# A convolution octet's inverse step joined to the next octet's forward steps, with ScalarE and VectorE each emptying one PSUM bank

## The chip, the cores and the metric

The kernel runs on one core of a Trainium2 chip. The metric is the device time of one launch in microseconds (us). Before the change it is 359.0 us, the median of three runs (358.95 to 359.44).

## The reference

Two branches share one layer norm and are added to the input. Branch A is a gated long convolution over the sequence, done in the reference by an FFT of twice the sequence length; branch B is a dense layer, Mish, and a second dense layer. There are S = 2048 rows, D = 448 channels and F = 1792 hidden columns, all in float32.

```python
def _A_ref(q, k, v, shift_k, ssm_k, ssm_D):
    k_pad = jnp.pad(k, ((0, 0), (ks - 1, 0), (0, 0)))
    k_shift = jnp.zeros_like(k)
    for t in range(ks):                                   # ks = 4
        k_shift = k_shift + k_pad[:, t:t + S, :] * shift_k[:, ks - 1 - t][None, None, :]
    kv = k_shift * v
    kv_f = rfft(pad(kv, to 2 * S), along S)
    kf_f = rfft(pad(ssm_k, to 2 * S))
    y = irfft(kv_f * kf_f)[:S]
    y = y + kv * ssm_D[None, None, :]
    return q * y

def _B_ref(x, w1, b1, w2):
    h = jnp.einsum("bsd,df->bsf", x, w1) + b1
    sp = jnp.log1p(jnp.exp(-jnp.abs(h))) + jnp.where(h > 0, h, jnp.zeros_like(h))
    act = h * jnp.tanh(sp)
    return jnp.einsum("bsf,fd->bsd", act, w2)

x = A_q
xn = _layernorm(x, axis=-1)
return x + _A_ref(xn, A_k, A_v, A_shift_k, A_ssm_k, A_ssm_D) + _B_ref(xn, B_w1, B_b1, B_w2)
```

## The kernel before

**The frame is branch B.** The sequence is cut into 8 chunks of 256 rows and the hidden columns into 7 pairs of 128, which gives 56 pairs. The program is written in slots, two to a pair. An even slot holds `g1_mm` (L494), the first dense layer of pair i: 22 matmuls of 128x256 that accumulate in one PSUM bank. An odd slot holds `mish` of that pair on ScalarE (L522), its split into a high and a low part (`ach` by a ScalarE cast, `acl` by a VectorE subtraction, L86 and L87), and `g2_mm` (L536), the second dense layer of the pair two before: 12 matmuls of 128x448. The order on every engine is the order in which the code is written. `at(slot, ...)` puts a step ahead of the slot's matmuls and `after(slot, ...)` behind them, and the loop over slots (L747) plays them in order. `dv()` lets one small waiting VectorE step through; `held` keeps a split back until `prod` calls it.

**Branch A is threaded through these slots** as a transform in steps of matmuls. Up to slot 59 the first transform step runs (L148), and its results go to DRAM (`Dh` for the filter, `Dkv` for the product of the shifted k and v). Slots 66 to 89 hold the middle step, in eight **octets** of frequencies, three slots apart (`OCT_AT`, L29), so that octets stand at even and odd slots in turn (66, 69, 72, ..., 87). Slots 100 and 108 hold the last step (L330).

An octet o consists of:

- **the forward steps**, called F(o) here: `f2_mm` (L231) four times, for the real and imaginary part of the filter (from the tile `ah`) and of the product (from `av`). One call is eight matmuls in tiles of 64x32 of the array, and each of them takes two passes, so it appears as 16 records in the trace (L237). A call fills a PSUM tile of two banks, r = 0 into the first and r = 1 into the second;
- **emptying the filter's two parts** into the SBUF tile `hs` (`h_out`), because VectorE reads only the product's parts from PSUM;
- **`prod`** (L252): four VectorE multiplications into `ya`, `yc`, `yb`, `yd` (L259), then `ya` minus `yb` (L264) and `yc` plus `yd` (L266);
- **the inverse step**, called I(o) here: `i1_mm` (L269), 16 matmuls in tiles of 32x64 with two passes each (L276), first all that read `ya`, then all that read `yc`. It fills two PSUM tiles, that is four banks;
- **`i1_out`** (L281): those four banks are emptied into `qe` and sent to the DRAM tensor `E` by a DMA of GpSimd's queue.

Three PSUM tiles of two banks serve the octets: `pp`, `pq`, `pr`, numbered 0, 1, 2. The tuples `hb`, `vb` and `ib` (L638) say which of them the filter's parts, the product's parts and the inverse step use. `GB` gives the single bank that a pair's `g1_mm` uses in these slots: bank 0 is the first of `pp`, bank 2 the first of `pq`, bank 4 the first of `pr`. `pg` is the pair of banks that `g2_mm` accumulates in. Before the change, F(o) stands at slot s of its octet and I(o-1) at slot s + 2 (at s + 1 for the last octet), and I(7) stands at slot 89.

Of the kernel before, what the change touches and what calls it, by code (L numbers as in the profile page):

```python
# [14 lines left out]
S, D, F = 2048, 448, 1792  # L15
# [5 lines left out]
NO = 8  # L21
# [23 lines left out]
def tile_kernel(ctx: ExitStack, tc, q, qT, k, v, sk, hT, sD, w10, w1, w2, c_fib, c_g, c_gi, c_i2, out):  # L45
    nc = tc.nc
    V = nc.vector
# [41 lines left out]
    def pc(n):  # L89
        return duo[n]  # L90
# [15 lines left out]
    def dv(n=1):  # L106
        for _ in range(n):
            if drip:
                drip.pop(0)()
# [4 lines left out]
    def at(slot, fn, *args):  # L114
        plan.setdefault(int(slot), []).append((fn, args))

    def after(slot, fn, *args):
        plan2.setdefault(int(slot), []).append((fn, args))
# [5 lines left out]
    HT, KR, VT, KV, PP, PS, ST, SD = {}, {}, {}, {}, {}, {}, {}, []  # L124
# [85 lines left out]
    GT, AH, AV, HS, Y = {}, {}, {}, {}, {}  # L210

    def t2(shape, name, bufs=1):
        if not sp2:
            ph1.close()
            sp2.append(ph2.enter_context(tc.tile_pool(name="ph2", bufs=1, reuse_waits="tile")))
        return sp2[0].tile(shape, F32, name=name, bufs=bufs)
# [14 lines left out]
    def f2_mm(a, o, c, n):  # L231
        p = pc(n)
        g = GT[o][0]
        for t in range(4):
            for r in range(2):
                rs = slice(64 * r, 64 * r + 64)
                nc.tensor.matmul(p[32 * t:32 * t + 32, r, :D], g[rs, t, c], a[rs, t], start=True, stop=True,  # L237
                                 tile_position=(64 * r, 32 * t))
        return p

    def hv_mm(o, hb, vb):
        PS["H", o] = [f2_mm(AH[o], o, c, hb[c]) for c in range(2)]
        h_out(o)
        PS["V", o] = [f2_mm(AV[o], o, c, vb[c]) for c in range(2)]
        AH.pop(o), AV.pop(o)

    def h_out(o):
        HS[o] = t2([128, 2, 2, D], "hs")
        for c, p in enumerate(PS.pop(("H", o))):
            nc.scalar.copy(HS[o][:, c], p[:, :, :D])  # L250

    def prod(o):  # L252
        vr, vi = (p[:, :, :D] for p in PS.pop(("V", o)))
        hs = HS.pop(o)
        hr, hi = hs[:, 0], hs[:, 1]
        a, c = Y[o] = [t2([128, 2, D], n, 2) for n in ("ya", "yc")]
        b, e = [t2([128, 2, D], n) for n in ("yb", "yd")]
        for x, *y in ((a, vr, hr), (c, vr, hi), (b, vi, hi), (e, vi, hr)):
            V.tensor_mul(x, *y)  # L259
        for fn in held:  # L260
            fn()
        held.clear()
        dv(2)
        V.tensor_sub(a, a, b)  # L264
        dv()
        V.tensor_add(c, c, e)  # L266
        dv()

    def i1_mm(o, ib):  # L269
        gi = GT[o][1]  # L270
        ps = [pc(n) for n in ib]
        for c in range(2):
            for t in range(4):
                ts = slice(32 * t, 32 * t + 32)
                for r in range(2):
                    nc.tensor.matmul(ps[t // 2][64 * r:64 * r + 64, t % 2, :D], gi[ts, r, c], Y[o][c][ts, r],  # L276
                                     start=c == 0, stop=c == 1, tile_position=(32 * t, 64 * r))
        PS["I", o] = ps
        Y.pop(o)

    def i1_out(o):  # L281
        qe = t2([128, 4, D], "qe") if o < NO - 1 else t2([128, 2, 2, D], "hs").rearrange("p a b d -> p (a b) d")
        for i, p in enumerate(PS.pop(("I", o))):
            nc.scalar.copy(qe[:, 2 * i:2 * i + 2], p[:, :, :D])  # L284
        for r in range(2):
            k = 8 * (o % 4) + 4 * r
            nc.gpsimd.dma_start(E.rearrange("p (k h) d -> p k h d", h=2)[:, k:k + 4, o // 4], qe[64 * r:64 * r + 64])  # L287
# [202 lines left out]
    AHL, P1, P2, GB = {}, {}, {}, {}  # L490
# [121 lines left out]
    for g, t in enumerate(KV_AT):  # L612
        d = t - (KV_AT[g - 1] if g else t - 6)
# [21 lines left out]
    at(OCT_AT[0], regroup)  # L635
    for o in range(NO):
        s, d = OCT_AT[0] + OCT_AT[1] * o, OCT_AT[1]
        hb, vb, ib = ((0, 1), (2, 0), (2, 1)) if s % 2 == 0 else ((2, 1), (0, 2), (0, 2))  # L638
        (at if o else after)(s - d if o else s - 7, o_load, AH, Dh, o, "ah")
        at(s - d - 1 if o else s - 3, o_load, AV, Dkv, o, "av")  # L640
        at(s, hv_mm, o, hb, vb)
        at(s, gi_load, o)
        after(s, prod, o)
        if s % 2:
            hv.add(s)
        if o == NO - 1:
            ib = 0, 1
        if o:
            at(s + (2 if o < NO - 1 else 1), i1_mm, o - 1, ib)
            after(s + (2 if o < NO - 1 else 1), i1_out, o - 1)  # L650
        if s % 2 == 0:
            GB[s // 2], GB[s // 2 + 1] = 2, 0
        else:
            GB[s // 2 + 1] = 2 if o < NO - 1 else 4
    at(s + 2, i1_mm, o, ib)
    after(s + 2, i1_out, o)
    GB[s // 2 + 2] = 5

    for t, (cs, load, folds, gates) in I2_AT.items():
        for m, (c, f) in enumerate(zip(cs, folds)):  # L660
# [56 lines left out]
    ps = [g2p.tile([128, 512], F32, name="pg2") for _ in range(2)]  # L717
# [114 lines left out]
```

## Time and profile before

| | |
|---|---|
| median of three runs | 359.0 us (358.95 to 359.44) |
| span of the profiled execution, first to last instruction | 357.0 us |
| TensorE busy | 351.0 us, 98% of the span |
| weight loads on TensorE | 289.5 us, 81% |
| VectorE busy | 270.6 us, 76% |
| ScalarE busy | 156.6 us, 44% |
| GpSimd busy | 70.3 us, 20% |
| octets (first matmul of F(0) to the first matmul behind I(7)) | 186.55 to about 284.9 us |

The page gives the span of one profiled execution. It has no separate total for that execution, so its own time is the span and what lies around it: the median of the runs is 2.0 us above the span, for start and end outside the recorded instructions. A time within the span is in microseconds from its start. In a row of the timeline the first number is the start, the second the duration, then come engine, line, operation, the tile written and the tiles read, and the number of instructions. Matmuls overlap in their pipeline, so the cost of a group of them is read from start to start, not from its duration.

### The profile page before, as it was taken

Reading aid. Unit: us, or ns where it says so; the run is one execution under the profiler, and the core shown is the slowest. Engines: PE = TensorE matmul, PEld = TensorE weight load, DVE = VectorE, ACT = ScalarE, POOL = GpSimd, SP = SyncE. Lnnn points to the kernel's source line nnn. Section 1 sums busy time; section 2 is a strip of 40 time slices with the busy share of each in tenths; the row PEclk is TensorE's granted clock in tenths of the full one; section 3 lists DMA queues with packets and bytes.
Section 4 is the critical chain, followed back from the end, with each engine's and each line's share of the span. In section 5 each row is a group of like instructions: output and inputs, shape, how many; then the busy total and the mean of one; then the engine's idle time right before and its main releaser. Section 6 shows DMA issues by size and latency. Waiting matters only on the chain.

```text
span 357.0 us, 7437 instructions
## 1 busy us (share of the span) xinstructions
PE 351.0 (98%) x3092; PEld 289.5 (81%) x3092; DVE 270.6 (76%) x375; ACT 156.6 (44%) x267; POOL 70.3 (20%) x78
## 2 busy tenths in 40 slices
PE   8999999999999999999999999999999999999995
PEld 2988888888888989888988757666775699979794
DVE  5989748999999999999437756756963933788941
ACT  4966552344243343343233454445445443354470
POOL 2037002822220240212000031011031116040030
PEclk9999999999999999999999999999999999999999
DMA  7998976949768637665869569999896387989086
GB/s 260 344 364 307 411 287 175 340 123 263 198 171 313 164 107 168 223 162 118 245 201 355 201 165 292 248 278 312 276 273 121 77 234 272 409 319 274 19 116 141
DMA packets 30691, 83.27 MB, mean 233 GB/s; under 512 B 3137, under 2 KB 15810, under 8 KB 30658
## 3 DMA queue, kind: packets, MB, share of 16 engines
q1 hardware_dynamic: 21842, 47.82, 39.4%
q0 software_dynamic: 4928, 22.95, 22.9%
q10 hardware_dynamic: 3888, 12.03, 12.8%
q8 instruction: 24, 0.39, 0.4%
q14 instruction: 9, 0.07, 0.1%
HBM read 54.34 MB, written 28.45 MB: 232 GB/s over the span
## 4 chain that ended last, share of the span: by engine, by line
PE 52%; issue 8%; DVE 6%; POOL 2%; DMA 1%
PE pq L514 7%; PE pg L546 7%; PE pg L548 7%; PE pg L547 6%; PE pp L514 5%; PE pr L514 4%; PE pp L237 3%; PE pr L237 3%; PE pp L276 2%; PE pg L514 2%; DVE x L201 2%; POOL x L184 2%; PE pq L237 2%; DMA xn<-in_qT_dram 1%; PE pr L276 1%
## 5 line engine op out<-in xcount | busy, mean ns | idle before, releaser
L546 PE MATMUL pg<-w2h,ach 128*128 128x448 f32 x224 | 82.5, 368 | 0.0
L548 PE MATMUL pg<-w2h,acl 128*128 128x448 f32 x224 | 81.4, 363 | 0.0
L547 PE MATMUL pg<-w2l,ach 128*128 128x448 f32 x224 | 81.2, 362 | 0.0
L87 DVE TENSOR_TENSOR acl<-a,ach 128x512 fp32r<-128x512 f32 x56 | 38.9, 695 | 31.7 <-ACT ach L86 31.5
L522 ACT ACTIVATE a<-pg,b1t 128x256 f32<-128x256 f32 x66 | 27.8, 472 | 65.4 <-PE pg L514 43.3
L514 PE MATMUL pg<-XH,w1h 128*128 128x256 f32 x264 | 52.6, 283 | 0.0
L546 PEld LDWEIGHTS pg<-w2h,ach 128*128 128x128 f32 x224 | 41.9, 187 | 11.5 <-issue 7.2
L514 PEld LDWEIGHTS pg<-XH,w1h 128*128 128x128 f32 x264 | 41.4, 188 | 6.9 <-issue 5.6
L547 PEld LDWEIGHTS pg<-w2l,ach 128*128 128x128 f32 x224 | 42.1, 188 | 2.4
L548 PEld LDWEIGHTS pg<-w2h,acl 128*128 128x128 f32 x224 | 42.1, 188 | 2.4
L514 PE MATMUL pg<-XL,w1h 128*128 128x256 f32 x264 | 42.9, 277 | 0.0
L158 DVE TENSOR_TENSOR st<-pq,st 128x896 f32<-128x896 f32 x32 | 34.8, 1089 | 4.8 <-ACT st L154 4.3
L514 PEld LDWEIGHTS pg<-XL,w1h 128*128 128x128 f32 x264 | 35.9, 188 | 0.0
L86 ACT CAST ach<-a 128x512 fp32r<-128x512 f32 x56 | 34.8, 622 | 1.7
L514 PE MATMUL pg<-XH,w1l 128*128 128x256 f32 x198 | 33.6, 278 | 0.0
L184 POOL TENSOR_TENSOR x<-kr,skb 128x896 f32<-128x896 f32 x8 | 17.0, 2123 | 70.9 <-PE pr L148 26.2
L514 PEld LDWEIGHTS pg<-XH,w1l 128*128 128x128 f32 x198 | 27.6, 188 | 0.2 <-DVE w1l L372 0.2
L201 DVE TENSOR_TENSOR x<-x 128x896 f32<-128x896 f32 x24 | 26.2, 1091 | 1.5 <-POOL x L184 0.8
L522 ACT ACTIVATE a<-pq,b1t 128x256 f32<-128x256 f32 x20 | 8.4, 471 | 31.8 <-PE pq L514 31.8
L287 POOL DMA_DIRECT2D E<-qe x14 | 8.7, 628 | 63.1 <-ACT qe L284 63.1
L154 ACT COPY st<-pr 128x896 f32<-128x896 f32 x16 | 14.5, 908 | 14.2 <-PE pr L148 12.3
L417 POOL TENSOR_TENSOR mv<-ve,mhalf 128x2 f32<-128x2 f32 x5 | 5.0, 1007 | 72.0 <-DVE ve L414 72.0
(138 smaller groups left out, 605.7 us busy)
## 6 DMA issues: line engine op xcount, KB each, us to landing
Dkv<-st ACTq DMA_DIRECT2D x16, 448.0 KB, 5.3
ah<-Dh SPq DMA_DIRECT2D x8, 896.0 KB, 7.5
av<-Dkv SPq DMA_DIRECT2D x8, 896.0 KB, 8.6
e<-E POOLq DMA_DIRECT2D x8, 896.0 KB, 7.2
E<-qe POOLq DMA_DIRECT2D x14, 448.0 KB, 5.9
kr<-in_k_dram SPq DMA_DIRECT2D x10, 448.0 KB, 6.8
Dh<-st ACTq DMA_DIRECT2D x10, 448.0 KB, 6.2
x<-in_hT_dram SPq DMA_DIRECT2D x8, 448.0 KB, 6.0
```

Of the source, the lines that this page charges most:

```text
L86: nc.scalar.copy(h, raw)
L87: V.tensor_sub(l, raw, h)
L154: nc.scalar.copy(st[:, 1], o)
L158: f(st[:, n], e, st[:, 1])
L184: nc.gpsimd.tensor_mul(o, KR[g - u // 2], skb[:, u:u + 1].to_broadcast([128, 2, D]))
L201: V.tensor_add(KV[g], KV[g], o)
L237: nc.tensor.matmul(p[32 * t:32 * t + 32, r, :D], g[rs, t, c], a[rs, t], start=True, stop=True, tile_position=(64 * r, 32 * t))
L514: nc.tensor.matmul(ps[n], l, r, start=all(m[0] != n for m in seq[:n_]), stop=all(m[0] != n for m in seq[n_ + 1:]))
L522: nc.scalar.activation(a[:, n], ps[n], AF.Mish, bias=b1t[:, 2 * p + n:2 * p + n + 1])
L546: nc.tensor.matmul(ps, ah[:, n, cs], w2h[:, f], start=f == 0, stop=False)
L547: nc.tensor.matmul(ps, ah[:, n, cs], w2l[:, f], start=False, stop=False)
L548: nc.tensor.matmul(ps, al[:, n, cs], w2h[:, f], start=False, stop=f == NF - 1)
```

## The change

I(o-1) is moved from slot s + 2 of octet o to the beginning of slot s, directly ahead of F(o), and the whole is one function, `octet`. The last inverse step, I(7), stays at slot 89 and is alone. Every PSUM tile of two banks that goes to SBUF (the two parts of the filter, the two results of the inverse step) is now emptied by `both`: ScalarE copies the first bank and VectorE the second, where ScalarE copied both before. `ya` and `yc` have one buffer instead of two. The bank numbers are dealt out anew: within a block the inverse step uses two of the three PSUM tiles, the filter's first part uses the third, its second part the inverse step's first tile, and so on.

```diff
-    def hv_mm(o, hb, vb):
-        PS["H", o] = [f2_mm(AH[o], o, c, hb[c]) for c in range(2)]
-        h_out(o)
+    def both(d, p):
+        nc.scalar.copy(d[:, 0], p[:, 0, :D])
+        V.tensor_copy(d[:, 1], p[:, 1, :D])
+
+    def octet(o, ib, hb, vb):
+        if o:
+            i1_mm(o - 1, ib)
+            i1_out(o - 1)
+        hs = HS[o] = t2([128, 2, 2, D], "hs")
+        ps = [f2_mm(AH[o], o, c, hb[c]) for c in range(2)]
+        for c in range(2):
+            both(hs[:, c], ps[c])
         PS["V", o] = [f2_mm(AV[o], o, c, vb[c]) for c in range(2)]
         AH.pop(o), AV.pop(o)
-
-    def h_out(o):
-        HS[o] = t2([128, 2, 2, D], "hs")
-        for c, p in enumerate(PS.pop(("H", o))):
-            nc.scalar.copy(HS[o][:, c], p[:, :, :D])
...
-        a, c = Y[o] = [t2([128, 2, D], n, 2) for n in ("ya", "yc")]
+        a, c = Y[o] = [t2([128, 2, D], n) for n in ("ya", "yc")]
...
-            nc.scalar.copy(qe[:, 2 * i:2 * i + 2], p[:, :, :D])
+            both(qe[:, 2 * i:2 * i + 2], p)
...
-        hb, vb, ib = ((0, 1), (2, 0), (2, 1)) if s % 2 == 0 else ((2, 1), (0, 2), (0, 2))
+        ib, hb, vb = ((0, 1), (2, 0), (1, 2)) if s % 2 == 0 else ((0, 2), (1, 0), (2, 1))
...
-        at(s, hv_mm, o, hb, vb)
+        at(s, octet, o, ib, hb, vb)
...
-        if o == NO - 1:
-            ib = 0, 1
-        if o:
-            at(s + (2 if o < NO - 1 else 1), i1_mm, o - 1, ib)
-            after(s + (2 if o < NO - 1 else 1), i1_out, o - 1)
-        if s % 2 == 0:
-            GB[s // 2], GB[s // 2 + 1] = 2, 0
+            GB[s // 2 + 1] = 0
         else:
-            GB[s // 2 + 1] = 2 if o < NO - 1 else 4
-    at(s + 2, i1_mm, o, ib)
+            GB[s // 2], GB[s // 2 + 1] = 0, 2
+    at(s + 2, i1_mm, o, (1, 2))
     after(s + 2, i1_out, o)
-    GB[s // 2 + 2] = 5
+    GB[s // 2 + 2] = 1
```

The line numbers of the changed kernel differ by a few: `i1_mm`'s matmuls are L280 there, `prod`'s multiplications L263, and the copies of `both` L242 (ScalarE) and L243 (VectorE).

On TensorE, before, octet 2 at slot 72 stands between the last matmul of one `g2_mm` and the first of a `g1_mm`. `ah` holds the filter, `av` the product, `g` the transform's weights.

```order
L548 MATMUL pg_2045<-w2h,acl 128x448
L237 MATMUL pp<-ah,g 32x448 x8
L237 MATMUL pq<-ah,g 32x448 x8
L237 MATMUL pr<-av,g 32x448 x8
L237 MATMUL pp<-av,g 32x448 x8
L514 MATMUL pq<-XH,w1h 128x256 x3
```

I(1) stood two slots later, at slot 74, in a place of its own.

On TensorE, in the changed kernel, the same place at slot 72:

```order
L552 MATMUL pg_2045<-w2h,acl 128x448
L280 MATMUL pp<-ya,gi 64x448 x4
L280 MATMUL pq<-ya,gi 64x448 x4
L280 MATMUL pp<-yc,gi 64x448 x4
L280 MATMUL pq<-yc,gi 64x448 x4
L237 MATMUL pr<-ah,g 32x448 x8
L237 MATMUL pp<-ah,g 32x448 x8
L237 MATMUL pq<-av,g 32x448 x8
L237 MATMUL pr<-av,g 32x448 x8
L518 MATMUL pp<-XH,w1h 128x256 x3
```

I(1) now stands directly ahead of F(2), and the second forward call writes `pp`, which I(1) filled just before.

On VectorE, before, octet 3 at slot 75: the two additions that empty `pg` into `qt`, then `prod`.

```order
L553 TENSOR_TENSOR qt<-pg_2045,qt 128x448
L259 TENSOR_TENSOR ya<-pp,hs 128x896
L259 TENSOR_TENSOR yc<-pp,hs 128x896
L259 TENSOR_TENSOR yb<-pr,hs 128x896
L259 TENSOR_TENSOR yd<-pr,hs 128x896
L87 TENSOR_TENSOR acl<-a,ach 128x512
L264 TENSOR_TENSOR ya<-ya,yb 128x896
L266 TENSOR_TENSOR yc<-yc,yd 128x896
```

On VectorE, in the changed kernel, the same place:

```order
L557 TENSOR_TENSOR qt<-pg_2045,qt 128x448
L243 COPY qe<-pp 128x448
L243 COPY qe<-pr 128x448
L243 COPY hs<-pq 128x448
L243 COPY hs<-pp 128x448
L263 TENSOR_TENSOR ya<-pr,hs 128x896
L263 TENSOR_TENSOR yc<-pr,hs 128x896
L263 TENSOR_TENSOR yb<-pq,hs 128x896
L263 TENSOR_TENSOR yd<-pq,hs 128x896
L87 TENSOR_TENSOR acl<-a,ach 128x512
L268 TENSOR_TENSOR ya<-ya,yb 128x896
L270 TENSOR_TENSOR yc<-yc,yd 128x896
```

Four copies out of PSUM stand ahead of the multiplications, two for the inverse step of the octet before and two for the filter; nothing else moved there.

## The prediction
> **What bounds the kernel now.** I read the page first, then what TensorE waited for, then the chain of work that ended last around one octet.
>
> ```profile
> span 357.0 us, 7437 instructions
> PE 351.0 (98%) x3092; PEld 289.5 (81%) x3092; DVE 270.6 (76%) x375; ACT 156.6 (44%) x267; POOL 70.3 (20%) x78
> ```
>
> A busy TensorE is not one at its peak, so the second view matters more: all that TensorE's matmuls waited for in the whole span (engine, line, the releaser, microseconds in total, times, longest).
>
> ```profile
> PE pg L696 <- DVE wz L692: 1.0, 1, 1.0
> PE pq L148 <- DVE x L204: 0.7, 1, 0.7
> PE pg L723 <- DVE ve L414: 0.2, 1, 0.2
> ```
>
> That is 1.9 us, none of it in the octets. TensorE is the bound from end to end, and a change to the octets can win only by shortening TensorE's own sequence there, and can lose by giving it a wait that it does not have. Now the chain from slot 70 to slot 72: pair 35's `g1_mm`, I(0), a `g2_mm`, F(2). A piece lasts from the end of the one before it to its own end.
>
> ```profile
> 203.16 2.51 PE pq L514 x22
> 205.67 0.54 PE pp L276 x4
> 206.20 0.03 PE pr L276 x4
> 206.23 0.35 PE pp L276 x4
> ...
> 207.33 0.03 PE pr L276 x4
> 207.36 0.40 PE pg L546
> 207.76 0.20 PE pg L547
> ...
> 209.97 0.91 PE pp L237 x16
> 210.88 0.75 PE pq L237 x16
> ```
>
> ```profile
> 213.13 2.70 PE pq L514 x22
> ```
>
> Every border between shapes costs something. I(0)'s first pass takes 0.54 where its later ones take 0.35 (entering: 0.19), and the first `g2_mm` matmul behind it takes 0.40 where the next takes 0.20 (leaving: 0.20). F(2)'s first call takes 0.91 where the second takes 0.75 (entering: 0.16), and the `g1_mm` behind it takes 2.70 where the one ahead took 2.51 (leaving: 0.19). An inverse step thus carries 0.39 us of borders and an octet's forward steps 0.35.
>
> **What the change removes.** Seven inverse steps, I(0) to I(6), lose their own place and stand directly ahead of F(1) to F(7). Each pair keeps I's entry and F's exit, and loses I's exit and F's entry: 0.20 + 0.16 = **0.36 us, seven times, 2.52 us**. What comes back is the new border inside the block and any new wait.
>
> **The new border.** No row shows a 32x64 tile followed by a 64x32 one. The bounds are nothing and the 0.20 of leaving an inverse step; I take 0.16, since the row nearest to it is the entry of these same forward matmuls. This leaves 0.20 a block. The Trainium skill, in TensorEngine Tiling, section Tiling Modes, Key Properties, says that changing the tiling mode, not just the tile, drains the array. By that rule the border between the two shapes still has its drain and the block saves 0.20; if switches between small tiles were free it would save 0.36 (rival C). The trace agrees in that all four borders above cost 0.16 to 0.20, but it has none of this kind.
>
> **The new wait.** The filter's second call now writes the tile that the inverse step filled just before it (`pp`), so it must wait for both copies out of it, and only one forward call stands in between. ScalarE's rows show when emptying starts:
>
> ```profile
> 207.40 0.91 ACT L284 COPY qe<-pp 128x896 f32<-128x896 f32 x1 [0.20 <-PE pr L276]
> 208.20 0.92 ACT L284 COPY qe<-pr 128x896 f32<-128x896 f32 x1
> 210.99 0.91 ACT L250 COPY hs<-pp 128x896 f32<-128x896 f32 x1 [1.87 <-PE pp L237]
> ```
>
> And TensorE's starts:
>
> ```profile
> 207.29 0.47 PE L546 MATMUL pg<-w2h,ach 128*128 128x448 f32 x1
> ...
> 209.90 0.98 PE L237 MATMUL pp<-ah,g 64*32 64x448 f32 x16
> 210.67 0.96 PE L237 MATMUL pq<-ah,g 64*32 64x448 f32 x16
> ```
>
> Put F where the `g2_mm` starts, at 207.29. Its second call is then due at 207.29 + 0.77 = 208.06 (0.77 from 209.90 to 210.67; its 0.16 entry lies in this). ScalarE starts at 207.40 and copies 448 columns: half of 0.91 is 0.45, and a copy of 512 out of PSUM takes 0.59:
>
> ```profile
> L478 ACT CAST XH<-pg 128x512 fp32r<-128x512 f32 x5 | 2.9, 587 | 6.9 <-PE pg L466 6.9
> ```
>
> so it ends between 207.85 and 207.99. VectorE has no copy of this kind. Its rows of 128x448 are:
>
> ```profile
> L553 DVE TENSOR_TENSOR qt<-pg,qt 128x448 f32<-128x448 f32 x16 | 9.3, 617 | 4.1 <-PE pg L548 4.1
> ...
> L421 DVE TENSOR_SCALAR xn<-qt,mv,rstd 128x448 f32<-128x448 f32 x2 | 1.0, 510 | 0.4 <-POOL rstd L417 0.4
> ```
>
> The first reads PSUM and has two inputs, the second has one input and reads SBUF; the copy lies between, 0.51 to 0.62, and I take the middle, 0.56. VectorE picks up a finished PSUM tile as fast as ScalarE or 0.05 later (212.56 below the start of its group at 211.42 is 1.14, ScalarE's 210.99 below 209.90 is 1.09). Its copy ends between 207.91 and 208.07.
>
> ```profile
> 212.56 1.09 DVE L259 TENSOR_TENSOR ya<-pr,hs 128x896 f32<-128x896 f32 x1 [3.88 <-PE pr L237]
> ```
>
> ```profile
> 211.42 0.96 PE L237 MATMUL pr<-av,g 64*32 64x448 f32 x16
> ```
>
> ```profile
> 211.94 0.39 PEld L237 LDWEIGHTS pp<-av,g 64*32 64x32 f32 x16 [0.36 <-ACT hs L250]
> ```
>
> A weight load follows the end of a ScalarE copy by 0.04 (210.99 + 0.91 to 211.94). A VectorE end is followed by 0.06 (167.13 + 1.09 to 168.28):
>
> ```profile
> 167.13 1.09 DVE L204 TENSOR_TENSOR x<-x 128x896 f32<-128x896 f32 x1
> 168.28 0.14 PEld L148 LDWEIGHTS pq<-x,con 32*64 32x64 f32 x2 [0.86 <-DVE x L204]
> ```
>
> So the weights of the second call can load between 207.97 and 208.13, against matmuls due at 208.06. The wait w is between nothing and, if the load's 0.1 lies wholly ahead of the matmul, about 0.2. With 0.56 for the copy the load comes at 208.02 to 208.07 and I take **w = 0.05**. The Trainium skill, in VectorE: DVE Perf Modes, section Why PSUM operands drop a tier, says that float32 out of PSUM gets no faster mode on VectorE; by that the copy is at the 0.62 end, w is nearer 0.1, and the sum below is 0.35 us smaller. The trace agrees as far as the 617 ns of L553 go; no row is a plain copy.
>
> Nothing else in a block waits: the third call uses the inverse step's other tile, emptied 0.5 us later for a call that comes 0.75 later, and the fourth uses the first call's tile, 1.5 us after that was filled. `hs` is complete before `prod` starts. VectorE gains four copies an octet, some 2.2 us, in time in which TensorE does not wait for it; ScalarE loses as much.
>
> **I(7) comes earlier against its data.** I(6) stood between F(7) and I(7); now only one `g2_mm` and one `g1_mm` do.
>
> ```profile
> 274.58 0.96 PE L237 MATMUL pp<-av,g 64*32 64x448 f32 x16
> ```
>
> ```profile
> 275.72 1.09 DVE L259 TENSOR_TENSOR ya<-pp,hs 128x896 f32<-128x896 f32 x1 [5.98 <-PE pp L237]
> ...
> 280.32 1.09 DVE L264 TENSOR_TENSOR ya<-ya,yb 128x896 f32<-128x896 f32 x1
> 281.32 1.08 DVE L266 TENSOR_TENSOR yc<-yc,yd 128x896 f32<-128x896 f32 x1
> ```
>
> From the start of the third forward call (274.58), `ya` is done at 281.41 and usable 6.89 later, `yc` at 282.40, usable 7.88 later. On TensorE the third call ends at 274.58 + 0.96 = 275.54 and the fourth 0.75 later; then a `g2_mm` takes 0.40 and eleven times 0.20, a `g1_mm` 2.51, and I(7) would be reached at 281.40, or, since a first matmul starts 0.07 ahead of its piece in the chain (209.90 against 209.97), at 281.33, 6.75 from the start of the third call. It waits 0.14 for `ya`, and half an inverse step (0.80) later 0.19 for `yc`: **0.33 us lost, once**. At the other octets another `g2_mm` or `g1_mm` of 2.5 us lies between, which covers it.
>
> **The sum.** 7 x (0.36 - 0.16 - 0.05) - 0.33 = 1.05 - 0.33 = 0.72 us. The span goes from 357.0 to 356.3, and with the 2.0 us around it the median from 359.0 to **358.3**. About 0.2%, 0.7 us, is what a measurement of this kernel can tell from no change, so the forecast lies on that border.
>
> **The rivals.**
>
> A is the forecast, w from 0 to 0.1: 7 x 0.20 - 0.33 = 1.07 down to 7 x 0.10 - 0.33 = 0.37, 357.9 to 358.6. Chance 0.55.
>
> B: the copies come at the late end and the loads lie wholly ahead of the matmuls, w from 0.1 to 0.2: a gain of 0.37 to a loss of 0.33, about 359.0. For it speaks the 617 ns row, against it that the first matmul at 168.28 starts with its weight load. Chance 0.20.
>
> C: the border inside the block is free. The second call would be due at 207.90, and the copies decide instead, at 207.97 to 208.03: 7 x 0.26 - 0.33 = 1.5 us gained, 357.5. Against it speak the four borders that all cost. Chance 0.13.
>
> D, slower: VectorE's half comes late. It has one queue in order, and the copies stand behind what was written ahead of them. TensorE waits at the second forward call in each block. Without a gain or loss is w = 0.15; above w = 0.26 the kernel is slower by over 0.7 us, and at w = 0.30 it is 360.0. The place where I see it nearest is octet 5 at slot 81, behind two norm steps that wait for a row from DRAM:
>
> ```profile
> 246.11 1.42 DVE L453 TENSOR_TENSOR xn<-xn,con 128x512 f32<-128x512 f32 x2 [1.01 <-DMA con<-MR]
> ```
>
> ```profile
> 237.45 0.50 SPq L447 DMA_DIRECT2D con<-MR  x1
> ```
>
> This row's load is queued on SP behind `ah`'s, which waits for the filter's calls of slot 78, and these now stand behind I(3): 1.7 us later (0.54 + 0.03 and three times 0.38), less the 0.4 gained by then. The norms would end near 248.9 and the block's copies are due near 249.0. Without that cover the one block loses what is over. Against D as a whole: VectorE idles 2 to 6 us ahead of `prod` in most octets (3.88 and 5.98 in the rows above). Chance 0.12.
>
> **How the numbers follow.** Faster by over 0.2%: C and some six tenths of A, 0.45. Slower: D, 0.12. Within: the rest, 0.43. The range cuts half of C and most of D away: 357.4 to 359.7.
>
> **What would show it.** In the chain after: the `g2_mm` or `g1_mm` behind the inverse step no longer takes 0.40 or 2.70 in its old place; the first L237 group behind L280 takes 0.91 (0.75 means C); the second group takes 0.75 + w; the waits of TensorE name L243 or L242 at the second call, and `ya` and `yc` at I(7) with 0.14 and 0.19. VectorE's copies show 0.51 to 0.62. The forecast is wrong if those copies start more than 0.1 behind ScalarE's, or if TensorE waits anywhere else between slots 66 and 89.

## The result and the profile after

The changed kernel takes **365.63 us** (median of five runs, 364.11 to 366.46) against 359.06 for the kernel before beside it: ratio 1.0181, 95% interval 1.0163 to 1.0199. It is slower by 6.6 us, where 0.7 us faster was forecast and the range ended at 359.7. The profiled execution has the median's time, and a span 6.8 us longer than before.

The first lines of the page after (busy time, share of the span, instructions of each engine):

```profile
span 363.8 us, 7475 instructions
PE 352.1 (97%) x3092; PEld 289.0 (79%) x3092; DVE 288.2 (79%) x407; ACT 145.5 (40%) x267; POOL 70.5 (19%) x78
```

TensorE is busy 1.1 us more; the other 5.7 us of the longer span are time in which it idles. What its matmuls waited for, and below it the longest wait of its weight loads (engine, line, releaser, microseconds in total, times, longest):

```profile
PE pp L237 <- DVE qe L243: 5.0, 7, 2.1
PE pg L694 <- DVE wz L690: 1.0, 1, 1.0
PE pq L148 <- DVE x L204: 0.7, 1, 0.7
PE pq L148 <- DMA x<-in_hT_dram: 0.3, 1, 0.3
PE pg L721 <- DVE ve L418: 0.3, 1, 0.3
PE pq L280 <- DVE ya L268: 0.2, 1, 0.2
```

```profile
PEld pp L237 <- DVE qe L243: 10.6, 7, 2.9
```

The first line is new: seven waits, one in each block, all at the second forward call into `pp`, all released by VectorE's half of emptying that tile. The chain of waits through octet 2 (start, duration, what) shows what such a wait is made of:

```profile
211.24 0.54 PE pp L280 x4
...
212.90 0.04 PE pq L280 x4
212.95 0.02 issue
212.97 0.54 ACT qe L242
213.51 0.02 issue
213.53 0.64 DVE qe L243
214.17 0.04 issue
214.21 0.99 PE pp L237 x16
215.20 0.75 PE pq L237 x16
```

The path leaves TensorE at the end of I(1), runs through ScalarE's copy **and then** VectorE's, and comes back 1.26 later. The same place in the timeline (start, duration, engine, line, tiles, count; in brackets the idle time ahead and its releaser):

```profile
212.97 0.53 ACT L242 COPY qe<-pp 128x448 f32<-128x448 f32 x1 [2.60 <-PE pq L280]
...
213.53 0.62 DVE L243 COPY qe<-pp 128x448 f32<-128x448 f32 x1 [1.49 <-ACT qe L242]
...
212.86 0.98 PE L237 MATMUL pr<-ah,g 64*32 64x448 f32 x16
214.21 0.99 PE L237 MATMUL pp<-ah,g 64*32 64x448 f32 x16 [0.37 <-DVE qe L243]
```

VectorE had been idle for 1.49 us, and its releaser is not TensorE but **ScalarE's copy** of the other bank. The two halves run one behind the other. The second call starts 1.35 behind the first, where 0.77 was due: a wait of 0.58, where the forecast had 0.05. The view of the waits counts only 0.37 of it at the matmul, since the weight load ahead of it waits too; starts of calls are the surer measure. They give 0.62 at octet 1 and 0.58 at octets 2, 3, 4 and 6. The prediction's own sign of being wrong has come true: VectorE's copy starts 0.56 behind ScalarE's (212.97 to 213.53), where it allowed 0.1. Two octets wait longer.

Octet 5 (VectorE's norms, its copy, and the two calls on TensorE):

```profile
252.04 1.43 DVE L457 TENSOR_TENSOR xn<-xn,con 128x512 f32<-128x512 f32 x2 [2.19 <-DMA con<-MR]
253.38 0.62 DVE L243 COPY qe<-pp 128x448 f32<-128x448 f32 x1
...
252.09 0.98 PE L237 MATMUL pq<-ah,g 64*32 64x448 f32 x16
254.06 0.99 PE L237 MATMUL pp<-ah,g 64*32 64x448 f32 x16 [0.98 <-DVE qe L243]
```

VectorE's copy stands behind two norm steps that wait for a row from DRAM; the second call comes 1.97 behind the first, a wait of 1.20. Octet 7:

```profile
280.59 0.53 ACT L242 COPY qe<-pp 128x448 f32<-128x448 f32 x1 [2.55 <-DMA E<-qe]
281.16 0.62 DVE L243 COPY qe<-pp 128x448 f32<-128x448 f32 x1 [4.28 <-ACT qe L242]
...
278.78 0.98 PE L237 MATMUL pq<-ah,g 64*32 64x448 f32 x16
281.84 0.99 PE L237 MATMUL pp<-ah,g 64*32 64x448 f32 x16 [2.07 <-DVE qe L243]
```

Here ScalarE's copy itself waits, for the write of the octet before out of `qe`, which has one buffer. In the chain of waits that write is one piece (start, duration, what):

```profile
268.44 12.05 DMA E<-qe
```

The second call comes 3.06 behind the first: a wait of 2.29.

Together 0.62 + 4 x 0.58 + 1.20 + 2.29 = 6.43 us at the second call, of the span's 6.8.

### The profile page after: what moved, and what is told of

It is laid out like the page before. It is cut to its first block, busy times and chain, and to the rows that moved or that the text cites. A ratio compares the mean times of both kernels' runs of the same rounds, so it can differ in the third digit from the quotient of the medians.

```text
span 363.8 us, 7475 instructions
## 1 busy us (share of the span) xinstructions
PE 352.1 (97%) x3092; PEld 289.0 (79%) x3092; DVE 288.2 (79%) x407; ACT 145.5 (40%) x267; POOL 70.5 (19%) x78
## 4 chain that ended last, share of the span: by engine, by line
PE 41%; issue 11%; DVE 7%; DMA 6%; POOL 2%; ACT 1%; POOLq 0%; ACTq 0%
PE pp L518 6%; PE pg L550 6%; PE pg L552 6%; PE pg L551 6%; PE pq L518 4%; DMA E<-qe 3%; DMA con<-MR 3%; PE pr L518 3%; PE pg L518 2%; PE pp L280 2%; PE pp L237 2%; POOL x L184 2%; DVE qe L243 1%; PE pr L237 1%; DVE x L201 1%
## 5 line engine op out<-in xcount | busy, mean ns | idle before, releaser
L526 ACT ACTIVATE a<-pp,b1t 128x256 f32<-128x256 f32 x24 | 10.1, 472 | 46.6 <-PE pp L518 43.0
L518 PE MATMUL pp<-XH,w1h 128*128 128x256 f32 x96 | 19.3, 283 | 0.0
```

The costliest lines, as they stand in the source:

```text
L518: nc.tensor.matmul(ps[n], l, r, start=all(m[0] != n for m in seq[:n_]), stop=all(m[0] != n for m in seq[n_ + 1:]))
L526: nc.scalar.activation(a[:, n], ps[n], AF.Mish, bias=b1t[:, 2 * p + n:2 * p + n + 1])
```

## The experiments

Two theories stood at first. S: the unit in which the program orders engines is the PSUM tile, and two engines that read one tile are put one behind the other, whichever banks they read. P: VectorE's copies are late because of what stands ahead of them on VectorE.

**ScalarE alone.** The joined block, with whole tiles emptied by ScalarE as before the change.

```diff
     def both(d, p):
-        nc.scalar.copy(d[:, 0], p[:, 0, :D])
-        V.tensor_copy(d[:, 1], p[:, 1, :D])
+        nc.scalar.copy(d, p[:, :, :D])
```

> The merged block as in the change, but ScalarE empties both banks of every PSUM tile in one copy of 128x896, as before the change; VectorE copies nothing. Theory S (the two half copies of one PSUM tile run one after the other, ScalarE 0.54 then VectorE 0.64, so a tile is empty 1.18 us after it is full): one copy of 0.91 is shorter, the second forward call starts 1.05 to 1.1 us behind the first instead of 1.35, with some 0.1 more at the third and fourth call; 7 x 0.15 = 1 us faster than the change, about 364.6. Rival P (the halves run side by side as meant, and what is late is VectorE's pick-up or the DMAs): ScalarE alone needs longer for four tiles, 1.35 stays or grows, 365.6 or more.

Measured: 361.49 us, ratio 1.0067 (1.0049 to 1.0085), better than the 364.6 expected. The timeline of octet 2:

```profile
212.28 0.98 PE L237 MATMUL pr<-ah,g 64*32 64x448 f32 x16
213.34 0.99 PE L237 MATMUL pp<-ah,g 64*32 64x448 f32 x16
214.15 0.99 PE L237 MATMUL pq<-av,g 64*32 64x448 f32 x16
```

One engine with twice the columns lets the second call start 1.06 behind the first; two engines on one tile took 1.35. The 4.1 us gained on the changed kernel are more than 0.3 a block, because the long waits of octets 5 and 7 went too. At octet 5, VectorE's queue no longer matters. At octet 7, the write out of `qe` that ScalarE's copy needs is issued 10.4 us ahead of that copy's turn in both kernels; here it lands 9.5 us after its issue, in the changed kernel it took 12.05 (268.44 to 280.49). Why it lands sooner no run shows.

**Tiles of one bank.** Each two-bank tile becomes two tiles of one bank, throughout the kernel; the same banks, the same split between the engines. Steps that read a whole tile are cut in two.

```diff
-    duo = [None] + [psp.tile([128, 2, 512], F32, name=n) for n in ("pq", "pr")]
+    duo = [None] + [Two([psp.tile([128, 512], F32, name=n + b) for b in 'ab']) for n in ("pq", "pr")]
...
         for x, *y in ((a, vr, hr), (c, vr, hi), (b, vi, hi), (e, vi, hr)):
-            V.tensor_mul(x, *y)
+            for r in range(2):
+                V.tensor_mul(x[:, r], y[0].t[r][:, :D], y[1][:, r])
```

> The changed kernel with the three PSUM tiles of two banks replaced by six tiles of one bank; instructions that read two banks at once are cut in two (the four multiplications of an octet become eight of 128x448, and the same in the first and last transform steps). VectorE's copy then waits for TensorE alone and not for ScalarE's copy. Theory S: in undisturbed blocks the second forward call starts 0.77 to 0.90 behind the first instead of 1.35, seven times some 0.5, less about 0.3 more wait at the last inverse step because the multiplications take longer: 362.0 to 362.8. Rival P: 1.35 stays, 365 to 366.

Measured: 359.41 us, ratio 1.0015 (1.0006 to 1.0025), below the 362.0 expected, which counted on the undisturbed blocks alone. Octet 2:

```profile
212.44 0.53 ACT L254 COPY qe<-ppa 128x448 f32<-128x448 f32 x1 [2.57 <-PE pqb L293]
...
212.50 0.63 DVE L255 COPY qe<-ppb 128x448 f32<-128x448 f32 x1 [1.01 <-PE pqb L293]
```

VectorE starts 0.06 behind ScalarE, and both are released by TensorE. The block's wait falls to about 0.04, and those of octets 5 and 7 go with it. S holds for the wait in each block. P does not explain it, for the copies stand at the same place of VectorE's queue here. Nor does the tile that the copies write: both still write one `qe`, and they run side by side.

**Two buffers of `qe`**, nothing else.

```diff
-        qe = t2([128, 4, D], "qe") if o < NO - 1 else ...
+        qe = t2([128, 4, D], "qe", 2) if o < NO - 1 else ...
```

> The changed kernel with two buffers for qe instead of one. If the long wait of octet 7 (2.29 us in the profile, ScalarE's copy into qe waiting for the write of qe to E of the octet before) is that buffer, the second forward call of F(7) starts 1.35 behind the first, and the kernel is 1.0 to 1.8 us faster than the change, 364.0 to 364.6. If the DMA engines are simply late and hold something else up, the wait moves to another place and the time stays at 365.6.

Measured: 363.27 us, ratio 1.0119 (1.0103 to 1.0135). This is 2.4 us better than the changed kernel, more than the 1.0 to 1.8 expected; in the traces octet 7 gives 1.70, and 0.47 comes from F(0), which starts earlier (186.67 against 187.14) ahead of the first use of `qe`. Octet 7's second call comes 1.36 behind the first as in the other octets; octet 5 stays:

```profile
251.66 0.98 PE L237 MATMUL pq<-ah,g 64*32 64x448 f32 x16
253.62 0.99 PE L237 MATMUL pp<-ah,g 64*32 64x448 f32 x16 [0.98 <-DVE qe L243]
```

**The row first.** The same with the load of octet 5's row put ahead of octet 4's block, so that on SP's queue it does not stand behind `ah`'s load.

```diff
-            at(b + at_["row"][jj], nt_row, c, jj)
+            if (c, jj) == (6, 1):
+                plan[b + at_["row"][jj]].insert(0, (nt_row, (c, jj)))
+            else:
+                at(b + at_["row"][jj], nt_row, c, jj)
```

> The change with two buffers of qe, and one row load (con of the second half of chunk 6) put ahead of octet 4's block in its slot, so that on SP's queue it no longer stands behind the load of ah, which waits for the block. If the norms that wait for this row are what holds octet 5's copies back, the row lands about 4 us earlier, the second call of octet 5 comes 1.35 behind the first as in the other octets, where it is 1.97 with two buffers alone, and the time is 0.6 better than 363.3: about 362.7. If something else holds them (the norms' own work, or the DMA's landing), octet 5 stays at about 1.9 and the time at 363.3.

Measured: 363.0 us, ratio 1.011 (1.0096 to 1.0124). The norms now run at 249.42, and octet 5 is like its neighbours:

```profile
251.76 0.98 PE L237 MATMUL pq<-ah,g 64*32 64x448 f32 x16
253.12 0.99 PE L237 MATMUL pp<-ah,g 64*32 64x448 f32 x16 [0.37 <-DVE qe L243]
```

In the trace 0.60 is gained there (1.96 became 1.36); in the median 0.3, within the two kernels' intervals. So the row's place on SP's queue, behind a block that had become longer, was octet 5's excess.

**Emptying by two engines alone.** The kernel before, with `both` and nothing else.

```diff
-            nc.scalar.copy(HS[o][:, c], p[:, :, :D])
+            both(HS[o][:, c], p)
...
-            nc.scalar.copy(qe[:, 2 * i:2 * i + 2], p[:, :, :D])
+            both(qe[:, 2 * i:2 * i + 2], p)
```

> The kernel before, with inverse and forward steps at their old places, and only the emptying changed: ScalarE the first bank, VectorE the second. Theory S: a tile is empty 1.18 us after it is full instead of 0.91, and the fourth forward call, which takes the first call's tile, waits 0.05 to 0.12 us in each of eight octets: 359.3 to 360.0. If the loss comes from moving the inverse step alone, 359.0; if the split alone carries it, 363 or more.

Measured: 361.74 us, ratio 1.0079 (1.0063 to 1.0095), more than expected. What TensorE waited for, the lines that before has not:

```profile
PE pp L280 <- DVE qe L249: 1.0, 1, 1.0
...
PE pr L237 <- DMA ah<-Dh: 0.4, 1, 0.4
```

The first is I(7): in the old order I(6)'s results are emptied after octet 7's products are written to VectorE's queue, so VectorE's half stands behind them, and I(7) needs that tile. The second is F(7), which waits 0.4 for the load of its filter. The fourth forward call also waits some 0.06 in each octet.

**Whole tiles, one to each engine.**

```diff
-    def both(d, p):
-        nc.scalar.copy(d[:, 0], p[:, 0, :D])
-        V.tensor_copy(d[:, 1], p[:, 1, :D])
+    def whole(i, d, p):
+        (V.tensor_copy if i else nc.scalar.copy)(d, p[:, :, :D])
```

> The merged block, in which ScalarE empties the whole of the first of each two PSUM tiles (128x896) and VectorE the whole of the second; no tile is shared. If the shared tile is what puts the copies behind each other, the two copies now overlap, the second forward call comes 1.07 behind the first as with ScalarE alone (0.30 late), and the third and fourth calls wait for nothing where with ScalarE alone they waited about 0.05 each: 7 x 0.1 better than that kernel's 361.5, about 360.7. If VectorE's queue is what is late, its whole copies (about 1.1 each) end later still, the third or fourth call waits for VectorE by 0.3 or more in each block, and the time is 363 or above.

Measured: 362.37 us, ratio 1.0093 (1.0076 to 1.0109): not the gain expected. Inside the block S's sign is right: no copy waits for the other engine, the second call comes 1.07 to 1.11 behind, and the third and fourth 0.75 to 0.78 (0.87 once, the third of octet 5). But the sum misses octet 7, where TensorE waits 1.0 us for ScalarE's copy, which the kernel with ScalarE alone did not have. The profile names the first forward call as what releases that copy, but the copy does not read that call's tile. The write out of `qe`, issued at 265.38, lands 11.3 later, and both engines' copies into `qe` start 0.1 behind that (276.80 and 276.82), as in the changed kernel; so the write is the likelier cause.

**One-bank tiles in the octets alone.** The kernel with one-bank tiles throughout started F(0) 0.8 late, from the cut steps ahead of the octets. Here the tiles are cut at slot 66 and joined again at slot 92.

```diff
+    class Two:
+        def __init__(s, n, p):
+            s.t = [p.tile([128, 512], F32, name=n + b) for b in "ab"]
...
-        duo[0] = g1p[0].tile([128, 2, 512], F32, name="pp")
+        duo[:] = [Two(n, g1p[0]) for n in ("pp", "pq", "pr")]
...
+    at(92, rejoin)
```

> The change with six PSUM tiles of one bank in the octets alone, so that the two engines never read one tile; the part ahead of the octets keeps its two-bank tiles, and the products are multiplied bank by bank. If the shared tile is the cause: both copies start together, the second forward call comes 0.77 to 0.81 behind the first, F(0) starts at 186.6 to 187.2 and not at 187.4, and the time is 358.3 to 359.0, under the 359.4 of the kernel with one-bank tiles throughout; what is left over the forecast is I(7)'s wait of 0.3 to 0.6. If the part ahead of the octets loses for another reason than its cut instructions, F(0) stays at 187.4 and the time at 359.4.

Measured: **358.82 us**, ratio 0.9997 (0.9989 to 1.0006), eleven runs. F(0) starts at 186.49. Octet 2's copies, and I(7):

```profile
211.55 0.53 ACT L258 COPY qe<-ppa 128x448 f32<-128x448 f32 x1 [2.57 <-PE pqb L297]
...
211.61 0.62 DVE L259 COPY qe<-ppb 128x448 f32<-128x448 f32 x1 [1.01 <-PE pqb L297]
...
282.95 0.59 PE L297 MATMUL pqa<-ya,gi 32*64 32x448 f32 x2 [0.18 <-DVE ya L285]
...
283.96 0.59 PE L297 MATMUL pqa<-yc,gi 32*64 32x448 f32 x2
```

This is the change as the forecast imagined it, and it ends level with before. From I(0) to I(6) it needs 75.34 us (197.25 to 272.59), before 75.74 from F(1) to F(7) (197.32 to 273.06): 0.40 gained in six octets, 0.07 each. I(7) gives 0.46 back: it starts 2.93 behind the `g1_mm` ahead of it (280.02 to 282.95), where 2.68 is enough when it waits for nothing (below, with the split behind the sums), so 0.25 late; and its second half follows 1.01 behind the first instead of 0.80.

**I(7) later.** The same with two buffers of `qe` and I(7) one slot later.

```diff
-    at(s + 2, i1_mm, o, (1, 2))
-    after(s + 2, i1_out, o)
+    at(s + 3, i1_mm, o, (1, 2))
+    after(s + 3, i1_out, o)
```

> The kernel with one-bank tiles in the octets, with two buffers of qe as well and I(7) one slot later (behind one more of the pairs' steps of 2.5 us). If I(7)'s wait for ya and yc is the forecast's 0.33 lost, it goes, and the time is 0.3 to 0.6 below the kernel with one-bank tiles in the octets: 357.8 to 358.5. If what I(7) feeds is on the path (its write to E, which the last transform step reads back), the gain is given back there as a wait of TensorE behind slot 92.

Measured: 360.22 us, ratio 1.0034 (1.0022 to 1.0046), worse, and by neither of the two ways. I(7) no longer waits; the `g2_mm` that now stands in its old place does (TensorE, then VectorE):

```profile
284.36 0.47 PE L567 MATMUL pg<-w2h,ach 128*128 128x448 f32 x1 [1.72 <-DVE qt L574]
...
283.68 1.15 DVE L574 TENSOR_TENSOR qt<-pg,qt 128x448 f32<-128x448 f32 x2
```

It needs `pg` empty, and the additions that empty it stand on VectorE behind the products and both sums of octet 7. I(7) in its old slot covered that.

**The split behind the sums.** One-bank tiles in the octets, and in the last octet `acl` behind `ya` and `yc` on VectorE.

```diff
+        last = o == NO - 1
-        for fn in held:
+        for fn in [] if last else held:
             fn()
...
         V.tensor_add(c, c, e)
+        if last:
+            for fn in held:
+                fn()
```

> The kernel with one-bank tiles in the octets, and in the last octet the split of a pair (acl, 0.60 us of VectorE from start to start) behind the two subtractions and additions that make ya and yc, instead of ahead of them. If I(7)'s wait is for VectorE's chain behind the third forward call, ya and yc come 0.6 earlier: I(7) starts where its turn is (282.65 in the trace of the kernel with one-bank tiles in the octets, where it started at 282.95), its second half follows 0.80 behind and not 1.01, and the time is 0.5 lower: 358.82 becomes about 358.3. If the split is then late for the matmuls that read acl, or the addition into qt that stands behind it is late for the next g2_mm as with I(7) in a later slot, TensorE waits there and nothing is gained.

Measured: 358.87 us, ratio 0.9991 (0.9982 to 1.0). The wait is gone: I(7) starts 2.68 behind the `g1_mm` ahead of it (280.69 to 283.37), and its halves are 0.80 apart. The time did not follow: in this profile F(0) starts at 186.91 (186.49 in the kernel without the edit), and octet 3's forward calls take 3.41 where the others take 3.23. Whether the half microsecond is there cannot be told from these runs; no kernel here is faster than before by more than 0.2%.

**Both engines in the old order, from one-bank tiles.** The kernel before, with `both` and one-bank tiles in the octets (and the products multiplied bank by bank, as above).

> The order of before (the inverse steps in their own places) with emptying by both engines from one-bank tiles in the octets. If the shared tile was the cost of splitting in the kernel with that part alone (361.74), it is gone: no wait at the fourth forward call nor at I(7), and the time is that of before, 359.1 within 0.3. The difference to the kernel with the joined block and one-bank tiles (358.82) is then what joining itself is worth, with its later I(7): by the forecast's terms without its wait 7 x 0.20 less 0.33 = 1.07, by the periods measured in that kernel (12.56 an octet against 12.62) about 0.3. If emptying by two engines costs in another way than by the shared tile, this one stays near 361.

Measured: 360.68 us, ratio 1.0047 (1.0035 to 1.006). The chain gives the forward steps 3.16 to 3.17 and the inverse steps 1.69 in every octet up to F(7), as before: emptying with two engines costs nothing there once no tile is shared. Against what was expected, I(7) waits still: VectorE's half of I(6)'s results starts 3.0 us behind ScalarE's, with no shared tile, only by VectorE's queue:

```profile
280.58 0.54 ACT L264 COPY qe<-ppa 128x448 f32<-128x448 f32 x1 [4.67 <-PE pqb L297]
...
283.60 0.61 DVE L265 COPY qe<-ppb 128x448 f32<-128x448 f32 x1
```

I(7) takes 3.24 (283.21 to 286.45) instead of 1.69, and these 1.55 are the 1.6 lost. With shared tiles in the old order I(7) lost as much: it was due at 285.33 and ended at 288.53, 1.51 late, of the 2.7 lost there. Here P, the queue on VectorE, is what holds. With what I(7) costs taken off both kernels, the medians leave 359.1 here and 358.4 in the joined block with one-bank tiles: joining itself is worth some 0.5 us (by the octets' starts) to 0.8.

## Why the prediction was wrong

**The step that failed** is the new wait, w = 0.05, in the sentence "VectorE picks up a finished PSUM tile as fast as ScalarE or 0.05 later". The rows behind it show VectorE as the only reader of its tile. In the changed kernel ScalarE reads the same tile, and VectorE's copy is released by ScalarE's copy and not by TensorE. So the two copies add, 0.53 and 0.62 with their gaps, and w is 0.58. With one-bank tiles the sentence is true to the hundredth (0.06 later), and so is the copy's bound of 0.62. The Trainium skill, in PSUM — Partial Sum Buffer, section PSUM bank collisions raise a hardware error, says that different banks may be used by two engines at once, and that accesses to be kept apart are those to one bank and quadrant, reads included. The runs agree that different banks can be emptied at the same time; the wait here came with the tile of two banks and went when it was cut. The traces name the releaser and the cut removes it; that the program's bookkeeping goes by tiles is the conclusion, and neither engine's copy was slower than alone.

**The waits of octets 5 and 7** were the rest, 1.20 and 2.29 us. Octet 5 was the place that rival D named, and its reckoning was near: norms ended by 248.9 and copies due at 249.0 (in the kernel with one-bank tiles in the octets the norms run from 247.44 to 248.87). But four blocks that were each some 0.6 longer carried the row's load to 241.93, from where it took until 252.04. Octet 7 was in no rival: the prediction says "Nothing else in a block waits", and the one buffer of `qe` was left out of that list. Rival D had the side right and the mechanism only at octet 5.

**What held.** In the trace of after:

- The new border: I(1) starts at 211.17 and F(2) at 212.86, 1.69 later, as a `g2_mm` started 1.69 behind I(0) before. The length of the first forward call can be read where the path stays on TensorE, in the chain of the kernel with one-bank tiles in the octets (its pieces are shorter, since the banks have names of their own):

```profile
211.54 0.49 PE pra L253
...
212.08 0.33 PE pra L253
...
212.45 0.33 PE ppa L253
```

  From 211.54 to 212.45 it takes 0.91, its 0.16 entry included. The border is not free (rival C), and 0.20 a block is saved.
- I(7) waits for `ya`, then for `yc`:

```profile
289.76 0.60 PE L280 MATMUL pq<-ya,gi 32*64 32x448 f32 x4 [0.23 <-DVE ya L268]
...
290.76 0.60 PE L280 MATMUL pq<-yc,gi 32*64 32x448 f32 x4
```

  The first half starts 2.99 behind its `g1_mm` (286.77), 0.31 late against the 2.68 of an I(7) that waits for nothing, and the second half follows 1.00 behind instead of 0.80. That is 0.51 for a term of 0.33.
- VectorE's copies take 0.61 to 0.62, the late end.

**The sum, mended.** -7 x 0.20 + 6.43 + 0.51 = 5.5. F(0) starts 0.6 later than before (187.14 against 186.55) and its fourth call comes 0.12 late, which gives 6.2 of 6.8. The rest, 0.6, goes for the most part to two small losses whose cause the runs do not show: the third call comes 0.77 to 0.78 behind the second and not 0.75, and three `g1_mm` (at 206.1, 232.2 and 286.8) take about 2.59 instead of 2.51, the first two at a granted clock of 1.00. F(0)'s start differs between 186.47 and 187.14 among the kernels with the same steps ahead of it, so part of the 0.6 ahead of the octets need not come from the change.

**Had only the shared tile been absent**, the forecast of 358.3 would have been 0.5 too low: w is 0.07 rather than 0.05 (the forward steps take 3.23, before 3.16), I(7) costs 0.46 rather than 0.33, and the slower `g1_mm`, 2.59 in that kernel too, comes on top.

## What to carry to other kernels

When a second engine is put on a tile, look for what releases each copy in the trace: two readers of one tile may be ordered by the program although they touch different banks, and then two engines are slower than one (1.35 against 1.06 here, 0.77 with a tile for each). Give each engine a tile of its own, and list for every copy on the new path both the engine's queue ahead of it and the buffer that it writes. A step that looks late may be covering the next wait: moving I(7) only passed 1.7 us to the `g2_mm` behind it.

## What the runs showed of the hardware

Two engines emptying neighbouring banks did not slow each other: 0.53 and 0.62 one behind the other as well as side by side. The switch from 32x64 to 64x32 tiles cost 0.16, as much as entering the same forward steps from full tiles.
